# The second layer of the last two passes as one block product of seven half-size products

## The chip, the cores and the metric

The kernel runs on one core of a Trainium2 chip. The metric is the time of one execution on the device in microseconds. The core has five engines that run at the same time, each its own list of instructions in order: TensorE (PE, matmuls; its weight loads are shown as PEld), VectorE (DVE), ScalarE (ACT), GpSimd (POOL) and SyncE (SP, which here issues DMAs only). They work on an on-chip memory of 128 partitions (SBUF) and on the accumulators of TensorE (PSUM), and wait for each other by semaphores.

## The reference

Attention within clusters over 4 batches x 8 heads x 768 tokens x 64 columns, then a feed-forward network on 3072 tokens x 512 columns. All is float32.

```python
q_assign = argmax(einsum(q_n, c_n));  k_assign = argmax(einsum(k_n, c_n))    # 16 clusters
scores = where(q_assign == k_assign, scale * q @ k.T, -1e9)
attn_out = softmax(scores) @ v
x = attn_out.transpose(0, 2, 1, 3).reshape(3072, 512)
h = x @ w_in                                       # 512 -> 2048
g = maximum(h, 0) + log1p(exp(-abs(h)))            # softplus
out = g @ w_out                                    # 2048 -> 512
```

## The kernel before

Each float32 factor is held as two fp16 parts, high and low, and each product is three matmuls: high by high, high by low, low by high. The work is cut into eight passes of 384 tokens (three tiles of 128). Passes 6 and 7 are the two halves of the last batch. The attention runs some passes ahead of the feed-forward network, and fills the time up to about 730 us on all engines.

In the feed-forward network of a pass, `ffn1` makes one block of 128 columns of the hidden layer for all 384 tokens (16 blocks `f`, 12 matmuls 128x384 each, L1219 to L1221) in a PSUM buffer `h`, of which there are two. `softplus` takes it from there: exp and ln on ACT (`fa`, L1240, L1241), then one DVE instruction for the maximum with h (`fg`, float32, L1252), which also frees the `h` buffer. Two blocks share one `fg` tile of 768 columns. Its high part is cast into `gh` by ACT or POOL (helper `cast`, L298), its low part is `fg` minus the high part, on POOL or DVE (L1272). `ffn2` has 24 matmuls 128x512 (L1303 to L1305) for each token tile and each half of `f`, with `gh` as stationary and `wo` (the weights of the second layer, high and low) as moving factor, into the one PSUM buffer `o`. DVE evicts it to `ot` (L1347 for the first half, L1352 for the second, which adds), and SP stores the tile. The last tile of pass 7 is made in two halves of 256 columns, each evicted and stored by itself (`last_tile`, `last_store`, L1325 to L1336). Every matmul has a weight load of its own ahead of it.

The order of all instructions is written out by hand. The generators of the kernel (`ffn1`, `ffn2`, `softplus`, ...) are channels; each pair of characters in the table `PLAN` names the channel whose next instruction is emitted. The table `SWAPPED` lists the instructions that go to the second of two possible engines (`either`). Waits between channels (`wait`, `ring`) only say what may be emitted when; on the chip the semaphores decide.

```python
for pi in passes: for f in range(NF): ffn1(pi, f)                  # one channel
for pi in passes: for half in 0, 1: for i in range(QT): ffn2(pi, half, i)   # another
```

Of the kernel before, what the change touches and what calls it, by code (L numbers as in the profile page):

```python
# [38 lines left out]
SWAPPED = ('g0_3', 'g0_5', 'g1_1', 'g2_5', 'g6_6', 'g6_7', 'g7_1', 'g7_2', 'g7_4', 'g7_7', 'gh1_6', 'gh2_4', 'gh3_1', 'gh6_7', 'gh7_0', 'gh7_2', 'gh7_3', 'gh7_5', 'gh7_6', 'gh7_7', 'k0_0', 'k0_1', 'k14', 'k18', 'k22', 'kT0_0_0', 'kT0_2_1', 'kT1_2_0', 'kT1_2_1', 'm12_2_0', 'm12_3_0', 'm20_4_0', 'm8_2_0', 'm8_3_0', 'p100', 'p101', 'p103', 'p136', 'p38', 'p39', 'p40', 'p42', 'p45', 'p46', 'p47', 'p59', 'p61', 'p64', 'p67', 'p71', 'p72', 'p79', 'p82', 'p85', 'p89', 'p90', 'p92', 'ph58', 'ph62', 'ph83', 'ph86', 'ph87', 'q0_0_0', 'qT1_1', 'u1', 'u11', 'u13', 'u21', 'u23', 'u27', 'u31', 'u33', 'u35', 'v8', 'vh14', 'vh18', 'w15', 'w19', 'w20', 'w23', 'w29', 'wh17', 'wh24', 'wh29', 'wh30', 'wh7', 'wh9', 'x0_2', 'x2_0', 'xh0_3', 'xh1_3', 'xh2_3', 'xh3_0', 'xh3_3', 'zk10', 'zk12', 'zk16', 'zk18', 'zk2', 'zk20', 'zk4', 'zq0_1', 'zq8_2')  # L39
# [39 lines left out]
    "7d7d7d0x0x0x0x0x0x0x0x0xczfs117dfsfs10d0767dd0ft0zft78cz7aczfufufufud0cz11fufq7f7f7f7f7fczfv11727h7h7h7h7h7h"
    "cz7j7j7jfv7ccz7e7e7e7e7l7lfw7l7l7ld0fw7j7j7lfv7n7n7n7e7e7ed01111117pfwfwd07p7p7n7pfx11111111111111cz7r7rczfy"  # L80
    "fyfy7g7ncz7iczfz7rfz7t7t7t7t7p7pfw11d07vcz117x7t7r7rfzfzfz7v7v7k7xczg0g0g07m7t7x7x7xcz7z7z7oczg1g1g17v7vd0g1"
    "g17z818181818112d07q7x7q7q7q7q7q7q7z7zd0g2838383cz7sczg3g3g312127u81cz85858383czg48585857w878787g4g4g4878712"
    "czd089898989897y85g4d08bczg5g58bg58b8b8b80d08289fx8282828d8d8d8d8d13828282121212d08f8f8f8f8f12g684cz8h8h8h8h"
    "8hczg7g7g7868dg2d08j8j8j1212121212128j8j121313d088cz8a8hczg8g88l8l8l8lg8d0cz8cczg98e158e8e8n8n8e8l8ng7g78n8n"
    "czd0gacz15gbgbgbg9g912138gd0g9g98p168p8p8e8p8p158ld0czd0cz8i8pgcgc1616d0gd138r8r8r8r8rgc8e8ed08t8t8t8t8tgc13"
    "131313gccz8v8kcz8v8m8tgegege1313d0cz8oczgf8vgf8v8q178q8q148q131316gfgf8vgfcz8x8xczghghghd08z8z8x8x8x8xd0gi8s"
    "ggcz91918z8zgg8z14141418cz17gj8qgjgj919191d0939316161616161616d08u919595czgj939797gj93938q8q959595czgkgkgk18"
    "8wcz8y95czglglgl99d09797cz16gm16gm9bd0gngn909718179b99czgogogo9999d0921a189292929292czglgl999b14141414czgpgp"
    "gp9d9d9d1b9dczd099czgqgq141414149bgp141414141a9d9b1b1bd0cz94d0grgq969dczgsgsgsgsd01898d018181818181818gp1a9f"
    "9f9f9f9fcz9h9h9h9h9h9a1b9219gid0gt9j9j9j9j9j9cczgugu9e1c9h9e9e9e9e9egt9e9l9l9l9l9l9ld0gv9n9n191919gucz9p9pd0"  # L90
# [17 lines left out]


class Order:  # L110
    BEGIN = {"PE": 1500.0, "DVE": 1600.0, "ACT": 2400.0, "POOL": 2700.0, "SP": 1190.0}
    LAT = {"PE": 200, "DVE": 60, "ACT": 60, "POOL": 60, "SP": 0}

    def __init__(self):
# [68 lines left out]
def tile_cluster_attention__then__softplus_ffn(  # L183
# [1021 lines left out]
    def ffn1(pi: int, f: int):  # L1205
# [18 lines left out]
        if f == NF - 1:  # L1224
            od.set(xkey[pi])
# [180 lines left out]
```

## Time and profile before

| | us |
|---|---|
| median of 3 runs (825.67 to 825.87) | 825.8 |
| span of the profiled execution | 825.4 |
| TensorE busy in it | 809.5 (98%) |
| TensorE weight loads | 525.8 (64%) |
| ScalarE busy | 537.0 (65%) |
| VectorE busy | 522.1 (63%) |
| GpSimd busy | 458.7 (56%) |

The profile is of one execution. A row of it names the engine, the line of the kernel (L1219), the operation, output and inputs by the program's names, and shapes as partitions x elements. Matmuls are pipelined, so the duration of one is longer than the distance to the next; the pace of a stream is read from start to start. A DVE or POOL row shows when the instruction began and ended, any standing still inside it included.

### The profile page before, as it was taken

How to read it: one execution, taken by the hardware profiler on the slowest of the kernel's cores; microseconds unless marked ns; L12 is line 12 of the kernel's file. 1: busy time of each engine (PE TensorE's matmuls, PEld its weight loads, DVE VectorE, ACT ScalarE, POOL GpSimd, SP SyncE). 2: the span in 40 equal slices, each digit the busy share in tenths (PEclk: the TensorE clock that was granted, in tenths of full speed). 3: DMA queues.
4: the chain of work that ended last, by engine and by line, in shares of the span. 5: the costliest groups of instructions: out<-in, count | busy, mean ns of one | idle time of the engine just before them, and what ended most of it. 6: DMA issues, size and time to landing. Idle time of an engine off the chain costs nothing.

```text
span 825.4 us, 19143 instructions
## 1 busy us (share of the span) xinstructions
PE 809.5 (98%) x7919; PEld 525.8 (64%) x7919; DVE 522.1 (63%) x909; ACT 537.0 (65%) x830; POOL 458.7 (56%) x341
## 2 busy tenths in 40 slices
PE   7999999999999999999989999999999999999998
PEld 7888987655666666566656656556666656655554
DVE  6789998877876877666785557577555444332222
ACT  5776789865877777558578677767766668622220
POOL 4753556444756576655667685677576666611120
PEclk9999999999999999999999999999999999999999
DMA  8986768999999999998799999999889787530001
GB/s 236 239 197 138 204 158 218 213 212 197 179 177 174 179 207 201 212 197 170 153 166 172 183 171 208 199 197 172 171 158 163 136 138 134 118 54 14 26 1 39
DMA packets 389816, 133.69 MB, mean 162 GB/s; under 512 B 367072, under 2 KB 382688, under 8 KB 389728
## 3 DMA queue, kind: packets, MB, share of 16 engines
q1 hardware_dynamic: 389728, 132.46, 81.3%
q8 instruction: 62, 1.02, 0.5%
q14 instruction: 26, 0.21, 0.1%
HBM read 35.68 MB, written 6.29 MB: 51 GB/s over the span
## 4 chain that ended last, share of the span: by engine, by line
PE 86%; DVE 5%; DMA 4%; ACT 2%; issue 1%; POOL 0%; SPq 0%; DVEq 0%; ACTq 0%; POOLq 0%
PE s L1064 11%; PE h L1219 9%; PE h L1221 9%; PE h L1220 9%; PE o L1303 9%; PE o L1305 9%; PE o L1304 9%; PE mbank L1144 5%; PE mbank L1150 3%; PE mbank L1148 3%; PE mbank L1149 3%; DMA pt<-phl 2%; DMA kt<-kn 1%; PE u L996 1%; PE u L997 1%; PE m L957 1%
## 5 line engine op out<-in xcount | busy, mean ns | idle before, releaser
L1100 POOL TENSOR_TENSOR phl<-p,phl 128x768 f16<-128x768 f32 x133 | 220.3, 1664 | 145.5 <-ACT phl L298 98.8
L1080 DVE TENSOR_REDUCE negm<-s 128x1 f32<-128x768 f32 x156 | 148.3, 953 | 57.3 <-PE s L1064 57.0
L1086 ACT ACTIVATE p<-s,negm 128x768 f32<-128x768 f32 x156 | 139.5, 895 | 68.7 <-DVE negm L1080 56.4
L1221 PE MATMUL h<-xT,wi 128*128 128x384 f16 x512 | 166.8, 326 | 0.0
L1220 PE MATMUL h<-xT,wi 128*128 128x384 f16 x512 | 166.7, 326 | 0.0
L1219 PE MATMUL h<-xT,wi 128*128 128x384 f16 x512 | 166.7, 325 | 0.1
L1303 PE MATMUL o<-wo,gh 128*128 128x512 f16 x376 | 142.4, 379 | 0.4 <-DVE ot L1352 0.4
L1305 PE MATMUL o<-wo,gh 128*128 128x512 f16 x376 | 142.5, 379 | 0.0
L1304 PE MATMUL o<-wo,gh 128*128 128x512 f16 x376 | 142.4, 379 | 0.0
L298 ACT CAST phl<-p 128x768 f16<-128x768 f32 x151 | 123.8, 829 | 19.2 <-DMA pt<-phl 16.3
L1252 DVE SCALAR_TENSOR_TENSOR fg<-fa,h 128x384 f32<-128x384 f32 x128 | 70.1, 549 | 103.9 <-ACT fa L1241 95.9
L1240 ACT ACTIVATE fa<-h 128x384 f32<-128x384 f32 x128 | 62.3, 487 | 111.0 <-PE h L1221 110.6
L1064 PE MATMUL s<-kt,qt 128*128 128x384 f16 x624 | 127.0, 326 | 2.4 <-ACT p L1086 2.4
L1272 POOL TENSOR_TENSOR gh<-fg,gh 128x768 f16<-128x768 f32 x54 | 89.3, 1657 | 29.5 <-ACT gh L298 28.2
L1148 PE MATMUL mbank<-vb,pt 128*128 128x65 f16 x936 | 101.3, 192 | 0.5 <-DMA pt<-phl 0.5
L1149 PE MATMUL mbank<-vb,pt 128*128 128x64 f16 x936 | 101.4, 192 | 0.0
L1150 PE MATMUL mbank<-vb,pt 128*128 128x65 f16 x936 | 101.0, 194 | 0.0
L1148 PEld LDWEIGHTS <-pt 128*128 128x128 f16 x936 | 86.9, 98 | 14.2 <-DMA pt<-phl 2.6
L1149 PEld LDWEIGHTS <-pt 128*128 128x128 f16 x936 | 86.3, 97 | 11.4
L1150 PEld LDWEIGHTS <-pt 128*128 128x128 f16 x936 | 86.5, 97 | 0.0
L1064 PEld LDWEIGHTS <-qt 128*128 128x128 f16 x624 | 58.3, 98 | 43.2 <-issue 3.1
L1221 PEld LDWEIGHTS <-wi 128*128 128x128 f16 x512 | 49.9, 98 | 33.2
(180 smaller groups left out, 1307.3 us busy)
## 6 DMA issues: line engine op xcount, KB each, us to landing
wo<-in_moe_w_in_dram SPq DMA_DIRECT2D x16, 512.0 KB, 5.4
wo<-in_moe_w_out_dram SPq DMA_DIRECT2D x14, 512.0 KB, 4.3
out_dram<-ot SPq DMA_DIRECT2D x23, 256.0 KB, 2.6
rawk<-in_k_dram SPq DMA_DIRECT2D x15, 384.0 KB, 4.2
rawq<-in_q_dram SPq DMA_DIRECT2D x15, 384.0 KB, 4.4
rawv<-in_v_dram SPq DMA_DIRECT2D x12, 384.0 KB, 4.0
rawv<-in_v_dram SPq DMA_DIRECT2D x8, 192.0 KB, 6.1
pt<-phl SPq DMA_TRANSPOSE x78, 5.9
```

Of the source, the lines that this page charges most:

```text
L1064: nc.tensor.matmul(st[:, j, :SH], qt[:, s, i], kt[:, s, NT // 2 * j : NT // 2 * (j + 1)], start=(s == 0), stop=(s == 1),)
L1080: yield op("DVE", 950, lambda: nc.vector.tensor_reduce(negm, st[:, :, :SH], AX.XY, ALU.max, negate=True))
L1100: lambda e: e.tensor_tensor(phl[:, u, 1], p32, phl[:, u, 0], ALU.subtract),
L1148: nc.tensor.matmul(av, pt[:, 0, c], vb[:, c, D : 2 * D + 1], start=(c == 0), stop=False)
L1149: nc.tensor.matmul(av[:, :D], pt[:, 0, c], vb[:, c, :D], start=False, stop=False)
L1150: nc.tensor.matmul(av, pt[:, 1, c], vb[:, c, D : 2 * D + 1], start=False, stop=(c == NT - 1))
L1219: nc.tensor.matmul(hp, w[0], x[0], start=(c == 0), stop=False)
L1220: nc.tensor.matmul(hp, w[0], x[1], start=False, stop=False)
L1221: nc.tensor.matmul(hp, w[1], x[0], start=False, stop=(c == NP - 1))
L1303: nc.tensor.matmul(po, g[0], wo[:, f, 0, 0], start=(f == f0), stop=False)
L1304: nc.tensor.matmul(po, g[0], wo[:, f, 0, 1], start=False, stop=False)
L1305: nc.tensor.matmul(po, g[1], wo[:, f, 0, 0], start=False, stop=(f == f0 + NF // 2 - 1))
```

## The change

The second layers of passes 6 and 7 become one product of 2 x 2 blocks. The blocks of the activations are A11 (pass 6, f 0 to 7), A12 (pass 6, f 8 to 15), A21 and A22 (pass 7 likewise); the blocks of the weights are halves of f by halves of 256 output columns. Instead of eight block products there are Strassen's seven:

```
M1 = (A11+A22)(B11+B22)   M2 = (A21+A22) B11       M3 = A11 (B12-B22)   M4 = A22 (B21-B11)
M5 = (A11+A12) B22        M6 = (A21-A11)(B11+B12)  M7 = (A12-A22)(B21+B22)
C11 = M1+M4-M5+M7   C12 = M3+M5   C21 = M2+M4   C22 = M1-M2+M3+M6
```

PE does them in the order M3, M5, M4, M1, M7, M2, M6, each with 72 matmuls 128x256 (`product`): token tiles 0 and 1 first, then tile 2. Pass 7 makes the blocks 8 to 15 of its first layer ahead of 0 to 7 (`blocks`).

What is new beside this: the sums of activations (`sum5`, `sum1`, `sum7`, `sum2`, `sum6`: for each of four pairs of f a float32 sum of 768 columns, a cast for its high part and a subtraction for its low part); the sums of weights (`form3`, `form4`, `form1`, `form76`: for each pair of f of M3, M4, M1, M7, M6 three additions of 512 columns, a cast and a subtraction); and the evictions, in which each product goes with its sign into one or two of the blocks c11, c12, c21, c22 (`scaled`, `plus`), each of which is stored in two pieces (`send`). The sums live in buffers that the attention no longer uses by then: raw inputs, keys, queries, values, transposed p, and others. Only A11 and A22 still get a high and a low part of their own. `last_tile` and `last_store` are gone, and so are the old second layers of passes 6 and 7. `PLAN` and `SWAPPED` are new tables; the planner's times and costs are dropped, and the number of idle matmuls that fill PE's early gaps stands in a table `FILL`.

```diff
-        if f == NF - 1:
+        if f == (NF // 2 - 1 if pi == len(passes) - 1 else NF - 1):
             od.set(xkey[pi])
...
+    def add(key, ns, slow, dst, a, b, o=ALU.add):
+        return either(
+            key, ("DVE", ns), ("POOL", slow), lambda e: e.tensor_tensor(dst, a, b, o), shared=True
+        )
+
+    def parts(key, m, j, src):
+        hi, lo = S[m, j][:, 0], S[m, j][:, 1]
+        yield cast(f"{key}h_{j}", 830, 1290, hi, src)
+        yield add(f"{key}l_{j}", 950, 1640, lo, src, hi, ALU.subtract)
+        od.set(("A", m, j))
...
+    def sum7(j):
+        yield wait("sum", 5, j)
+        yield from six("qt", 2, ("last", "pt"), 7, j)
+        t = F[0, 1, j]
+        yield add(f"S7_{j}", 950, 1640, t, t, F[1, 1, j], ALU.subtract)
+        od.set(("sum", 7, j))
+        yield from parts("S7", 7, j, t)
+        od.set(tiles7[f"a12_{j}k"])
...
+    def form(m, j, a, b, o):
+
+        k = yield from ring("fg", 2)
+        t = flat(p2.tile([P, 2, nb], F32, tag="fg", name=f"t{m}_{j}"))
+        high = t[:, : 2 * HE].rearrange("p (u e) -> p u e", u=2)
+        low = t[:, 2 * HE : 3 * HE].bitcast(F16).rearrange("p (u e) -> p u e", u=2)
+        yield add(f"T{m}a_{j}", 640, 1160, high, a[0], b[0], o)
+        yield add(f"T{m}b_{j}", 340, 1160, low, a[1], b[1], o)
+        yield add(f"T{m}c_{j}", 640, 1160, high, high, low)
+        to = T[m, j]
+        yield cast(f"T{m}h_{j}", 655, 890, to[:, 0], high)
+        yield add(f"T{m}l_{j}", 640, 1160, to[:, 1], high, to[:, 0], ALU.subtract)
+        od.set(("T", m, j))
+        od.set(k)
...
+                    for u in range(2):
+                        x = [g[:, s, u, i * P : (i + 1) * P] for s in range(2)]
+                        first, last = i % 2 + j + u == 0, i > 0 and j == NJ - 1 and u == 1
+                        nc.tensor.matmul(to, x[0], t[0][:, u], start=first, stop=False)
+                        nc.tensor.matmul(to, x[0], t[1][:, u], start=False, stop=False)
+                        nc.tensor.matmul(to, x[1], t[0][:, u], start=False, stop=last)
...
+        for m in (1, 7, 2, 6):
+            key, x = yield from bank(ps_s, "s", 2, f"m{m}")
+            for w in range(2):
+                yield from product(m, w, x[:, w])
+                od.spawn(out41726(b, m, w, x[:, w], key if w else None))
...
-    def last_tile(pi, i):
-        b, c0 = passes[pi]
-        for e in range(2):
...
-    od.spawn((y for pi in range(len(passes)) for f in range(NF) for y in ffn1(pi, f)))
-    od.spawn((y for pi in range(len(passes)) for half in range(2) for i in range(QT) for y in ffn2(pi, half, i)))
+    od.spawn((y for pi in range(len(passes)) for f in blocks(pi) for y in ffn1(pi, f)))
+    od.spawn((y for pi in range(len(passes)) for y in (layer2(pi) if pi < R1 else seven(pi))))
+    for gen in (form3(), form4(), form1(), form76(), accs3()):
+        od.spawn(gen)
```

The order is the same in both kernels, on every engine, up to about 628.3 us of the trace. Behind it, VectorE's list in the second layer of pass 7 reads so before (`o_3_0_1` is the product of token tile 3 of batch 3, second half; `fg_7_2` the third pair of blocks of pass 7):

```order
L1252 SCALAR_TENSOR_TENSOR fg_7_2_11296<-fa_7_4_11292,h_7_4_11261 128x384
L1352 SCALAR_TENSOR_TENSOR ot_3_0_11118<-o_3_0_1_11253,ot_3_0_11118 128x512
L1252 SCALAR_TENSOR_TENSOR fg_7_2_11296<-fa_7_5_11325,h_7_5_11293 128x384
L1252 SCALAR_TENSOR_TENSOR fg_7_3_11360<-fa_7_6_11356,h_7_6_11326 128x384
L1352 SCALAR_TENSOR_TENSOR ot_3_1_11186<-o_3_1_1_11317,ot_3_1_11186 128x512
```

Each of these waits for PE or for ACT. After, at the fg rows of blocks 14 and 15 of pass 7, the list reads so (`pa2` is the pair of blocks in a dead buffer of transposed p; `s1_...` a sum or low part of M1's activations, `a12_2` the sum of M7, `t7_1` and `t1_3` sums of weights, `vb3` the place of M1's fourth block of weights, `c12` a block of the result):

```order
L1247 SCALAR_TENSOR_TENSOR pa2_11402<-fa_7_14_11458,h_7_14_11404 128x384
L1247 SCALAR_TENSOR_TENSOR pa2_11402<-fa_7_15_11472,h_7_15_11459 128x384
L1587 SCALAR_TENSOR_TENSOR c12_10936<-m35_11218,c22_10878 128x512
L1349 TENSOR_TENSOR s1_0_11337<-s1_1_11499,s1_0_11337 128x768
L1349 TENSOR_TENSOR vb3_110<-t1_3_11368,vb3_110 128x512
L1349 TENSOR_TENSOR a12_2_11039<-a12_2_11039,pa2_11402 128x768
L1349 TENSOR_TENSOR t7_1_11523<-kt1_11055,kt4_9918 128x512
L1349 TENSOR_TENSOR s1_2_11526<-na2_10548,pa2_11402 128x768
```

Between the fg rows there now stand rows of 128x768 and 128x512 whose inputs are both in SBUF. On GpSimd the list ended before with the parts of pass 7's activations:

```order
L298 CAST gh_7_6_11594<-fg_7_6_11554 128x768
L298 CAST gh_7_5_11525<-fg_7_5_11491 128x768
L1272 TENSOR_TENSOR gh_7_6_11594<-fg_7_6_11554,gh_7_6_11594 128x768
L1272 TENSOR_TENSOR gh_7_5_11525<-fg_7_5_11491,gh_7_5_11525 128x768
L298 CAST gh_7_7_11653<-fg_7_7_11649 128x768
```

After, it ends with sums and low parts of activations for M6 and M2 (`s6`, `s5`) and of weights for M6 (`t6`):

```order
L1349 TENSOR_TENSOR s6_0_11701<-ra0_10263,s6_0_11701 128x768
L276 CAST s5_0_10931<-pa0_11295 128x768
L1349 TENSOR_TENSOR s5_0_10931<-pa0_11295,s5_0_10931 128x768
L1349 TENSOR_TENSOR t6_1_11837<-kt1_11055,nt1_9616 128x512
L1349 TENSOR_TENSOR s5_2_11054<-pa2_11402,s5_2_11054 128x768
L1349 TENSOR_TENSOR t6_3_11928<-vb3_110,vb1_106 128x512
L1349 TENSOR_TENSOR t6_3_11928<-t6_3_11928 128x512
```

The subtractions and casts of pass 7's last pairs have left the list, and a sum that DVE and ACT go on with stands at its end.

## Rows read from the trace of the kernel before

**Rows 1.** The page, parts 1 and 2: busy us, share, instructions; 40 slices in tenths.
```profile
PE 809.5 (98%) x7919; PEld 525.8 (64%) x7919; DVE 522.1 (63%) x909; ACT 537.0 (65%) x830; POOL 458.7 (56%) x341
PE   7999999999999999999989999999999999999998
```
**Rows 2.** The page, part 4: the chain that ended last, by engine.
```profile
PE 86%; DVE 5%; DMA 4%; ACT 2%; issue 1%; POOL 0%; SPq 0%; DVEq 0%; ACTq 0%; POOLq 0%
```
**Rows 3.** Stretches: us, busy of PE, PEld, DVE, ACT, POOL; PE clock, DMA share, GB/s.
```profile
100.00:200.00 100.00, 99.47 (x932) 67.36 (x931) 82.20 (x149) 73.74 (x119) 48.76 (x39) 1.00 0.93 206
...
628.30:718.00 89.70, 89.70 (x871) 54.91 (x870) 41.64 (x67) 61.42 (x90) 54.21 (x35) 1.00 0.74 132
718.00:759.00 41.00, 41.00 (x279) 22.24 (x277) 11.26 (x19) 12.84 (x24) 8.75 (x8) 1.00 0.26 45
759.00:822.00 63.00, 63.00 (x348) 33.87 (x346) 14.65 (x23) 11.97 (x23) 9.51 (x8) 1.00 0.06 24
```
**Rows 4.** Timeline of PE, 800.9 to 822.4 us: start, duration, operation.
```profile
800.96 0.33 PE L1219 MATMUL h<-xT,wi 128*128 128x384 f16 x1
...
801.77 0.33 PE L1221 MATMUL h<-xT,wi 128*128 128x384 f16 x1
801.93 0.38 PE L1303 MATMUL o<-wo,gh 128*128 128x512 f16 x1
...
807.77 0.38 PE L1303 MATMUL o<-wo,gh 128*128 128x512 f16 x1
...
816.83 0.27 PE L1325 MATMUL o<-wo,gh 128*128 128x256 f16 x1
...
821.96 0.27 PE L1327 MATMUL o<-wo,gh 128*128 128x256 f16 x1
```
**Rows 5.** Timeline of DVE, its last row; in brackets the idle time before.
```profile
822.27 0.42 DVE L1335 SCALAR_TENSOR_TENSOR ot<-o,ot 128x256 f32<-128x256 f32 x1 [2.19 <-PE o L1327]
```
**Rows 6.** Timelines of ACT and DVE after that first-layer block.
```profile
802.13 0.49 ACT L1240 ACTIVATE fa<-h 128x384 f32<-128x384 f32 x1 [3.50 <-PE h L1221]
802.65 0.52 ACT L1241 ACTIVATE fa<-fa 128x384 f32<-128x384 f32 x1
...
803.27 0.56 DVE L1252 SCALAR_TENSOR_TENSOR fg<-fa,h 128x384 f32<-128x384 f32 x1 [4.04 <-ACT fa L1241]
```
**Rows 7.** Groups of DVE by shape, 740 to 825.4: count | busy us, mean ns | idle before.
```profile
L1252 DVE SCALAR_TENSOR_TENSOR fg<-fa,h 128x384 f32<-128x384 f32 x16 | 8.8, 553 | 33.4 <-ACT fa L1241 33.4
L1272 DVE TENSOR_TENSOR gh<-fg,gh 128x768 f16<-128x768 f32 x5 | 4.8, 957 | 4.9 <-ACT gh L298 4.6 <-POOL gh L298 0.4
L1352 DVE SCALAR_TENSOR_TENSOR ot<-o,ot 128x512 f32<-128x512 f32 x5 | 3.5, 692 | 15.5 <-PE o L1305 15.5
...
L1335 DVE SCALAR_TENSOR_TENSOR ot<-o,ot 128x256 f32<-128x256 f32 x2 | 0.8, 425 | 4.1 <-PE o L1327 4.1
```
**Rows 8.** Groups of DVE, then POOL, by shape: 128x512 and 128x768 subtractions, casts.
```profile
L426 DVE TENSOR_TENSOR wo<-wo 128x512 f16<-128x512 f32 x4 | 2.7, 684 | 0.0
...
L426 POOL TENSOR_TENSOR wo<-wraw,wo 128x512 f16<-128x512 f32 x2 | 2.3, 1160 | 1.9 <-ACT wo L298 1.8
...
L1272 POOL TENSOR_TENSOR gh<-fg,gh 128x768 f16<-128x768 f32 x15 | 24.6, 1644 | 4.5 <-ACT gh L298 3.3 <-PE o L1305 1.1
...
L298 POOL CAST gh<-fg 128x768 f16<-128x768 f32 x7 | 6.3, 909 | 65.2 <-DVE fg L1252 65.2
```
**Rows 9.** Timelines of DVE and POOL at 143 and 300 us; all of L1100 on DVE.
```profile
143.53 2.68 DVE L1100 TENSOR_TENSOR phl<-p,phl 128x768 f16<-128x768 f32 x3
...
300.41 2.12 DVE L1100 TENSOR_TENSOR phl<-p,phl 128x768 f16<-128x768 f32 x1
...
300.09 1.64 POOL L1100 TENSOR_TENSOR phl<-p,phl 128x768 f16<-128x768 f32 x1
...
L1100 DVE TENSOR_TENSOR phl<-p,phl x23: 943/956/2147, 143.5 to 508.1; 128x768 f16<-128x768 f32 x23
```
**Rows 10.** Groups of PE's weight loads, 816.8 to 822.3.
```profile
L1326 PEld LDWEIGHTS <-gh 128*128 128x128 f16 x16 | 1.6, 98 | 0.3
```
**Rows 11.** The tile pt (transposed p): time of its DMAs from issue to landing.
```profile
DMA to landing us min/median/max: 5.4/5.9/7.8
```

More of the change, by code (lines that the diff above doesn't have):

```diff
@@ L269, in tile_cluster_attention__then__softplus_ffn, with warm @@
     idle = mbank[:, 512 - WARM :]
-    def warm(gap):
-        if gap > WARM_FROM:
-            cold = min(gap * WARM_SHARE, max(0.0, COLD - cold_for[0]))
-            cold_for[0] += cold
-            for _ in range(int(cold / 100 + (gap * WARM_SHARE - cold) / 52)):
-                nc.tensor.matmul(idle, eye, ones[:, :WARM], start=True, stop=True)
-    cold_for = [0.0]
+    def warm(times):
+        for _ in range(times):
+            nc.tensor.matmul(idle, eye, ones[:, :WARM], start=True, stop=True)
     od.warm = warm
@@ L754, in prep_q @@
         n1 = p2.tile([P, c12, P], F16, name=f"qn1_{sfx}", **early)
+        if n == LAST - 3 and pi == len(passes) - 1:
+            od.set(("raws", "q"))
         if n == 0 and pi == 0:
@@ L797, in prep_q @@
             n2k, n2 = (yield from ring("n2", 1)), N2
+            if n == LAST - 3 and pi == len(passes) - 1:
+                od.set(("n2", "last"))
             if n == H:
@@ L1274, in softplus, with blocks @@
         )
-        od.set(fk)
-        od.set(("g", pi, fp))
+        if fk:
+            od.set(fk)
+        od.set(("g", pi, fp))
+        if pi == R1 + 1:
+            od.set(("A", 4, fp - NJ))
+            od.spawn(sum1(fp - NJ))
+            od.spawn(sum7(fp - NJ))
+        elif pi == R1:
+            od.set(("A", 3, fp))
+    R1 = len(passes) - 2
+    NJ = NF // 4
+    HE = DM // 2
+    def blocks(pi):
+        return list(range(NF)) if pi <= R1 else list(range(NF // 2, NF)) + list(range(NF // 2))
@@ new lines, in layer2, with flat, as_sum, as_form @@
+    def layer2(pi):
+        for half in range(2):
+            for i in range(QT):
+                yield from ffn2(pi, half, i)
+    F, S, T, tiles7 = {}, {}, {}, {}
+    def flat(ap):
+        n = len(ap.shape) - 1
+        axes = " ".join("abcde"[:n])
+        return ap.rearrange(f"p {axes} -> p ({axes})") if n > 1 else ap
+    def as_sum(ap):
+        return ap.rearrange("p (s u t) -> p s u t", s=2, u=2)
+    def as_form(ap):
+        return ap[:, : 4 * HE].rearrange("p (s u e) -> p s u e", s=2, u=2)
@@ new lines, in parts, with six @@
+    def parts(key, m, j, src):
[3 more added lines that the diff above has]
+        od.set(("A", m, j))
+    def six(tag, size, event, m, j, slots=2):
+        if j % 2 == 0:
+            yield wait(*event)
+            yield from take(tag, size, f"s{m}_{j}", [P, 4, 2 * nb], F16, **({"bufs": NP} if tag == "kt" else {}))
+            for u in range(2):
+                S[m, j + u] = as_sum(flat(tiles7[f"s{m}_{j}"][:, 2 * u : 2 * u + 2]))
+            od.set(("room", m, j))
+        else:
+            yield wait("room", m, j - 1)
@@ new lines, in form3 @@
+    def form3():
+        yield wait("raws", "q")
+        for u in range(2):
+            yield from take("n1", N1, f"nt{u}", [P, 6 * HE], F16, bufs=N1)
+            T[3, u] = as_form(tiles7[f"nt{u}"])
+        od.set(("form", "n1"))
+        yield wait("raws", "v")
+        for j in range(NJ):
+            if j >= 2:
+                yield from ring("vb", NP)
+                T[3, j] = as_form(flat(VB[j - 2]))
+            if j == NJ - 1:
+                od.set(("form", "vb"))
+            yield from form(
+                3, j, [weight(0, 1, j, s) for s in range(2)], [weight(1, 1, j, s) for s in range(2)], ALU.subtract
+            )
@@ new lines, in three, with form4 @@
+    def three(m, key):
+        for j in range(3):
+            T[m, j] = as_form(flat(tiles7[key])[:, 4 * HE * j : 4 * HE * (j + 1)])
+    def form4():
+        yield wait("kn", LAST - 1)
+        yield from take("kt", NP, "kt4", [P, 12 * HE], F16, bufs=NP)
+        three(4, "kt4")
+        od.set(("kt", 0))
+        yield wait("form", "vb")
+        yield from ring("vb", NP)
+        T[4, 3] = as_form(flat(VB[2]))
+        od.set(("form", "vb2"))
+        for j in range(NJ):
+            yield from form(
+                4, j, [weight(1, 0, j, s) for s in range(2)], [weight(0, 0, j, s) for s in range(2)], ALU.subtract
+            )
@@ new lines, in form1, with form76 @@
+    def form1():
+        yield wait("room", 5, 2)
+        yield from take("kt", NP, "kt1", [P, 12 * HE], F16, bufs=NP)
+        three(1, "kt1")
+        yield wait("form", "vb2")
+        yield from ring("vb", NP)
+        T[1, 3] = as_form(flat(VB[3]))
+        for j in range(NJ):
+            yield from form(
+                1, j, [weight(0, 0, j, s) for s in range(2)], [weight(1, 1, j, s) for s in range(2)], ALU.add
+            )
+    def form76():
+        yield wait("xT", len(passes) - 1)
+        yield from take("xT", 2, "xt7", [P, 12 * HE], F16)
+        three(7, "xt7")
+        yield wait("accs")
+        yield from take("ot", QT, "ot7", [P, 4 * HE], F16, bufs=QT)
+        T[7, 3] = as_form(tiles7["ot7"])
+        for m, other in ((7, 4), (6, 3)):
+            for j in range(NJ):
+                if m == 6:
+                    yield wait("done", 3)
+                    T[6, j] = T[3, j]
+                yield wait("T", 1, j)
+                yield wait("T", other, j)
+                yield from form(
+                    m, j, [T[1, j][:, s] for s in range(2)], [T[other, j][:, s] for s in range(2)], ALU.add
+                )
@@ new lines, in tile_cluster_attention__then__softplus_ffn, with span, scaled, emit @@
+    C = {}
+    def span(w):
+        return slice(0, 2) if w == 0 else slice(0, 1)
+    def scaled(key, dst, src, size, w):
+        def emit(e):
+            if e is nc.scalar:
+                e.activation(dst, src, AF.Copy, scale=size)
+            else:
+                e.tensor_scalar(dst, src, size, None, ALU.mult)
+        return either(key, ("ACT", 570 if w == 0 else 350), ("DVE", 680 if w == 0 else 360), emit)
+    def plus(dst, src, acc, w, sign=1.0):
+        return op(
+            "DVE",
+            360 if w else 680,
+            lambda: nc.vector.scalar_tensor_tensor(dst, src, sign / SW2, acc, ALU.mult, ALU.add),
+        )
@@ new lines, in send, with accs3 @@
+    def send(b, row, e, w, acc):
+        c0 = passes[R1 + row][1]
+        to = out_v[b, :, c0 : c0 + 2, e * HE : (e + 1) * HE] if w == 0 else out_v[b, :, c0 + 2 : c0 + 3, e * HE : (e + 1) * HE]
+        return op("SP", 60, lambda: nc.sync.dma_start(to, acc), dma=(128e3 if w else 256e3) / 290)
+    def accs3():
+        yield wait("last", "p32")
+        for r, e in ((2, 2), (1, 2), (1, 1)):
+            yield from take("p32", 3, f"c{r}{e}", [P, QT, HE], F32, bufs=3)
+            t = tiles7[f"c{r}{e}"]
+            C[r, e, 0], C[r, e, 1] = t[:, :2], t[:, 2:]
+            od.set(("c", r, e))
```

377 lines of the change are left out of this document (261 added, 116 removed).

## The prediction

> **What bounds the kernel now.** I read the page's busy shares and its 40 slices first: the reader is to see that TensorE (PE) is busy 98% of the span, in every slice but the first, and that no other engine is above 65% [rows 1]. The chain of the page's fourth part agrees: 86% of it is PE [rows 2]. Then the table of stretches, cut where the change cuts: instructions stand in the same order on every engine up to about 628.3 us, and from there to 822 us PE is busy without a gap, at a granted clock of 1.00 (the 2.4 GHz level), while VectorE (DVE) has 41.6 of 89.7 us, then 11.3 of 41.0, then 14.7 of 63.0 [rows 3]. So at the end PE alone sets the time and DVE is nearly idle. What the change takes from PE is gain, as long as what it gives to DVE fits. That is the whole question.
>
> **Term 1, PE.** The timeline of PE gives the pace of each shape, from start to start. First layer, 128x384: 801.77 − 800.96 over five steps, 0.162 us. Second layer, 128x512: 816.83 − 807.77 over 42 steps, 0.2157 us. The last tile, 128x256: 821.96 − 816.83 over 47 steps, 0.1091 us [rows 4]. Of the last two passes' second layers, before has 12 groups of 24 matmuls less the last tile's group, 264 x 0.2157 = 56.9 us, plus 48 x 0.1091 = 5.2, together 62.2 us. After has seven products of 72 matmuls 128x256: 504 x 0.1091 = 55.0 us. That is **−7.15 us** (seven eighths of the work, plus the fixed 2 x 109.1 − 215.7 = 2.5 ns that a halved matmul pays again). The 192 more matmuls bring 192 more weight loads; one takes 98 ns [rows 10] and lay hidden under the 109 ns matmuls of the last tile, so I cost them at nothing; uncovered they are a rival below. The end is of the same shape in both: last 128x256 group, one DVE eviction of 0.42 us, one store of 128 KB, end 3.44 us after the last matmul's start [rows 4, 5]. With PE never waiting the span would be 825.4 − 7.15 = 818.2 us.
>
> The Trainium skill, "TensorE: Matmul & The Clock Gate", section "Back-to-back issue gap", speaks against the change: it states that a stream of load and matmul pairs sustains about 131 ns at 512 columns and 81 ns at 128, where the load counts beside the columns. As an estimate on a line between these, 256 columns would take 98 ns, and the halving would cost 504 x 98 − (264 x 131 + 48 x 98) = +10 us. The trace has 215.7 and 109.1 ns for such streams [rows 4], so I go by the trace.
>
> **Term 2, what DVE must do, and with GpSimd (POOL).** From the place where the orders part, DVE has 106 instructions before (65.5 us by the prices below) and 222 after (156.6 us): the sums of activations (128x768) and of weights (128x512), and evictions into four blocks of the result. Prices: 128x768 with both inputs in SBUF 0.957, an fg row 0.553, a 128x512 eviction 0.692, a 128x256 one 0.425 [rows 7], a 128x512 subtraction 0.684 on DVE, 1.16 on POOL, where the 128x768 one takes 1.64 [rows 8].
>
> Two more readings of rows. Three 128x768 subtractions in a row took 2.68 us, not 3 x 0.956 = 2.87: independent DVE instructions overlap, 0.09 us for each after the first [rows 9]. And the subtraction at 300.41 took 2.12 us; POOL's own, begun at 300.09, ended at 301.73, and DVE's ended 0.80 later: it stood still while POOL worked, but for about 0.15 us [rows 9]. So such an instruction on one of the two engines stops the other.
>
> The stretch that decides runs from the fg row of block 15, the last of the eight first-layer blocks that pass 7 now does first (PE ends that block at 758.0 if it never waits), to the fourth block of weights of the last product, M6, which PE wants at 810.9. In it DVE has, by the order, 24 sums 128x768 (23.0 us), 25 of 128x512 (17.1), 8 fg rows (4.4), 5 large and 6 small evictions (3.5 + 2.6): **50.5 us**. With 0.09 off for some 60 of them, 45.1. POOL has nine instructions in it: 4 x 1.64 + 4 x 1.16 + one cast of 0.91 = 12.1 us; less 9 x 0.15 that is 10.8, and as 40.0 of DVE's 50.5 us (79%) are of the kind that is stopped, 8.5 us are added. DVE needs **53.6 us**. PE gives it 96 first-layer matmuls x 0.162 + 342 of the products x 0.1091 = 52.9, less 1.9 from the end of a first-layer block to the end of its fg row (exp, ln, DVE: 801.93 to 803.83 [rows 4, 6]), 51.0. So DVE comes **2.6 us late**, and PE waits for it in the last third, either before first-layer blocks (the ring of two PSUM buffers, freed by fg rows that stand in DVE's queue behind sums) or before M2 and M6. The bounds: if POOL takes nothing from DVE, not late (0); if nothing overlaps, 50.5 + 8.5 = 59.0, 8 late. I take the overlapped value, since the row with three such subtractions is the nearest to what stands there.
>
> The stretch before, 718 to 759 us, has 56 DVE instructions of 38.8 us, overlapped 34.5, with POOL's share 41.9 us, against 41.8 that PE gives: 0 to 0.7 late. From 628 to 718, the attention's end, DVE has 92 instructions of 64 us, about 76 of the 90 us with what POOL stops; the stretch 100 to 200 us of the trace had DVE at 82.2 and PE still at 99.47 of 100 [rows 3], so such a load costs PE some 0.5 us in 100. For both I take **+0.5**, bounds 0 and 4, the upper one because the transposes of p have a landing time of 5.4 to 7.8 us [rows 11] and their inputs now queue on DVE behind weight sums.
>
> Rest of the edits: the planner's constants removed and the idle matmuls from a table move nothing (200 of them in both); pass 7's blocks in another order cost nothing on PE; one result store more goes through SP in a stretch with a DMA share of 6% [rows 3]. Of the sums, those on ScalarE (casts) lie beside: 104 us of ACT in 190.
>
> **Sum.** Span 825.4 − 7.15 + 2.6 + 0.5 = 821.35. The median of the runs is 825.8, 0.4 above the profiled span, so **821.8 us**. The bounds of the terms: 818.2 + 0 + 0 and 818.2 + 8 + 4, that is 818.6 to 830.6 as times.
>
> **Rivals.** (1) *DVE keeps up*: POOL's instructions meet mostly DVE's waits, or PSUM evictions that they don't stop, so less than 5 of the 8.5 us are added. For it: PE had waits of nearly nothing with DVE at 82% [rows 3]. Against: here DVE would be needed for all of the 51 us. Time 818.6 to 819.5. (2) *Slower*: DVE becomes the bound outright. Most of the added instructions are chains in which the next reads what the last wrote (a + b, c + d, their sum, cast, low part), and each such step may wait for the end of the one before; then the full durations count, 59 us against 51, and 0.7 to 3 us come in the stretch before. PE loses 8 to 11 us, more than the 7.15 it saved; from 7.15 us of lateness on the change is a loss. Time 826.6 to 829.6, middle 828. For it: the place of DVE's instructions is fixed by the order, so a late cast stops everything behind it. Against: chains are interleaved in the order. (3) *The attention's end stalls*: the subtractions that make p's low part stand on DVE behind weight sums, transposes start later, PE waits for pt; 1 to 4 us over the forecast, 823 to 826. For it: the landing times [rows 11]. (4) *The change does not save what it says*: the pace at 128 x 256 rests on 48 matmuls; were the 98 ns load [rows 10] exposed for the 192 more, +18.8 us, 837. Against: those 48 [rows 4]. The skill's rule above belongs here.
>
> **How the numbers follow.** Chances: forecast (820 to 824) 0.46; rival 1 0.20; rival 2 0.18; rival 3 0.12; rival 4 0.02; 0.02 for anything else. About 0.2% (1.65 us) is what a measurement of this kernel can tell from no change: faster is below 824.1, slower above 827.5. Faster: 0.43 of the forecast + 0.20 + 0.04 of rival 3 = 0.67. Same: 0.03 + 0.06 of rival 2 + 0.08 of rival 3 = 0.17. Slower: 0.12 of rival 2 + 0.04 = 0.16. For 8 in 10 the range goes from just under rival 1, 818.0, to the middle of rival 2, 828.0: 0.1 lies above, and up to 0.1 below or in what I have not thought of.
>
> **What would show it.** Term 1: three lines of 168 matmuls each at 109 ns from start to start, and the same 3.4 us after the last. Term 2: PE idle of some 3 us between 740 and 811, its releaser the fg row or a sum on DVE, and DVE busy over 85% there; sums of 128x768 that last 1.1 to 2.1 us where POOL works. PE at 100% there would mean rival 1; PE idle of 7 us and more, with DVE's gaps in chains of weight sums, rival 2; PE idle before 718 with a DMA of pt as releaser, rival 3. The forecast is wrong at its root if PE waits for ScalarE's casts, which I cost at nothing.

## The result: slower, by waits for evictions

The changed kernel takes 833.5 us (median of six runs), the kernel before 825.4 us (median of six): a ratio of 1.0099, 95% interval 1.0085 to 1.0114. That is slower, and above the range of the prediction (818 to 828).

First the page of the changed kernel, busy times and three of the rows of 40 slices, which answer to [rows 1]:

```profile
PE 806.6 (97%) x8111; PEld 546.6 (66%) x8111; DVE 610.5 (73%) x1025; ACT 551.1 (66%) x854; POOL 472.0 (57%) x354
PE   8999999999999999999999999999999999999967
DVE  6788998877876877666765546586555778889973
PEclk9999999999999999999999999999999999999989
```

VectorE (DVE), 2 tenths busy at the end before, is now at 8 and 9 there, and TensorE (PE) has holes in the last slices. The table of stretches (length, then busy time of PE, weight loads, DVE, ACT, POOL, then PE's granted clock, DMA share, GB/s) answers to [rows 3]:

```profile
628.00:718.00 90.00, 90.00 (x869) 54.71 (x868) 67.89 (x96) 55.26 (x84) 53.92 (x42) 1.00 0.74 135
718.00:758.00 40.00, 40.00 (x348) 28.98 (x346) 36.31 (x55) 19.76 (x36) 15.10 (x12) 1.00 0.18 37
758.00:800.00 42.00, 39.79 (x313) 30.30 (x311) 40.62 (x55) 21.07 (x38) 11.41 (x7) 1.00 0.01 1
800.00:808.00 8.00, 1.03 (x8) 0.64 (x7) 7.25 (x10) 3.44 (x5) 3.18 (x2) 0.77 0.00 0
808.00:812.00 4.00, 4.00 (x24) 2.92 (x23) 0.61 (x2) 0.00 (x0) 0.00 (x0) 0.60 0.47 164
812.00:829.00 17.00, 14.84 (x136) 13.00 (x134) 7.05 (x10) 0.62 (x1) 1.74 (x1) 1.00 0.14 47
```

Up to 758 us PE is as full as before. From 758 to 800 it loses 2.2 us, from 800 to 808 nearly all, and behind that hole the granted clock is low (0.50, the 1.2 GHz level, from 807.3 to 811.2 us). The table of PE's waits from 628 us on (who waited for whom: total, times, longest) says for what:

```profile
PE m L1522 <- DVE c L1587: 9.1, 3, 7.0
PE h L1210 <- DVE fg L1247: 2.0, 3, 0.9
PE m L1524 <- DVE gh L1274: 0.2, 1, 0.2
```

The three large ones are waits of a product's matmul for an eviction (`c`, L1587). PE's timeline shows them at three places; in brackets the idle time before the row:

```profile
800.13 0.27 PE L1524 MATMUL m<-xt,s 128*128 128x256 f16 x1
807.37 0.37 PE L1522 MATMUL m<-xt,s 128*128 128x256 f16 x1 [6.97 <-DVE c L1587]
...
817.97 0.27 PE L1522 MATMUL m<-wo,s 128*128 128x256 f16 x1 [1.38 <-DVE c L1587]
...
826.77 0.27 PE L1522 MATMUL m<-nt,s 128*128 128x256 f16 x1 [0.78 <-DVE c L1587]
```

They are the products of token tile 2 of M7, M2 and M6. Their operands are there: `xt` and `s7` had served tiles 0 and 1 just before. What the matmul at 807.37 waits for is the row at 806.64 of DVE's timeline, the eviction of M7's tiles 0 and 1:

```profile
799.39 0.95 DVE L1349 TENSOR_TENSOR pa<-pa,fg 128x768 f32<-128x768 f32 x1
800.25 0.95 DVE L1349 TENSOR_TENSOR s<-pa,s 128x768 f16<-128x768 f32 x1
801.12 0.68 DVE L1587 SCALAR_TENSOR_TENSOR c<-m,c 128x512 f32<-128x512 f32 x1
801.75 1.71 DVE L1349 TENSOR_TENSOR nt<-t,nt 128x512 f16<-128x512 f32 x1
803.50 1.03 DVE L1349 TENSOR_TENSOR t<-kt,vb 128x512 f32<-128x512 f16 x2
804.56 0.69 DVE L1349 TENSOR_TENSOR t<-t 128x512 f32<-128x512 f32 x1
805.17 0.95 DVE L1349 TENSOR_TENSOR n<-fg,n 128x768 f32<-128x768 f32 x1
806.04 0.68 DVE L1349 TENSOR_TENSOR vb<-t,vb 128x512 f16<-128x512 f32 x1
806.64 0.68 DVE L1587 SCALAR_TENSOR_TENSOR c<-m,c 128x512 f32<-128x512 f32 x1
811.39 0.42 DVE L1587 SCALAR_TENSOR_TENSOR c<-m,c 128x256 f32<-128x256 f32 x1 [4.07 <-PE m L1524]
```

DVE has no gap of more than 0.04 us from 799.39 to the end of that eviction; the eviction comes when its turn comes, behind sums for M2 and M6, which PE makes only after M7. Each such product has one PSUM tile, token tiles 0 and 1 in its first half, tile 2 in its second. In PE's list of the changed kernel a wait for DVE (for a count of its semaphore `DVE_49`) stands ahead of the first matmul of tile 2 that the program issues after that eviction:

```
L1522 MATMUL m7_11814<-xt7_11175,s7_0_11338 128x256 [waits DVE_49]
L1522 MATMUL m2_11972<-wo_120,s5_0_10931 128x256 [waits DVE_49]
L1522 MATMUL m6_12057<-nt0_9615,s6_0_11701 128x256 [waits DVE_49]
```

For M2 and M6 that is the first matmul of tile 2, for M7 the seventh. The six ahead of it, the last at 800.13, stand before the eviction in the program and have no such wait: they write the second half while the first is still full.

**The account.** The first 600 us are the same list in both kernels, yet the traces differ by up to 2.6 us there from one execution to the next. So I count from a mark in the part that is common, the DVE row `negm` at 612.81 us of the kernel before, which stands at 613.00 in the changed one. From it to the end are 212.58 us before and 219.64 after, +7.1. The account: 7.15 us less work on PE; the waits above, 9.1 + 2.0 + 0.2 = 11.3; for each of the seven some 0.16 us more, since idle time counts from the modelled end of a matmul (0.27 us after its start) where the next could have started after 0.11, together 1.1; and the low clock, in these two rows of PE's timeline 3.20 us for 15 steps, 0.213 us where the others have 0.109, on 18 matmuls 1.9 us:

```profile
807.75 0.42 PE L1524 MATMUL m<-xt,s 128*128 128x256 f16 x1
...
810.95 0.40 PE L1524 MATMUL m<-ot,s 128*128 128x256 f16 x1
```

−7.15 + 11.3 + 1.1 + 1.9 = +7.2.

### The profile page after: what moved, and what is told of

The parts are those of the page before. It is cut to its first block, busy times and chain, and to the rows that moved or that the text cites. A ratio compares the mean times of both kernels' runs of the same rounds, so it can differ in the third digit from the quotient of the medians.

```text
span 832.6 us, 19674 instructions
## 1 busy us (share of the span) xinstructions
PE 806.6 (97%) x8111; PEld 546.6 (66%) x8111; DVE 610.5 (73%) x1025; ACT 551.1 (66%) x854; POOL 472.0 (57%) x354
## 4 chain that ended last, share of the span: by engine, by line
PE 59%; DVE 8%; DMA 6%; ACT 2%; issue 1%; POOL 0%; DVEq 0%; ACTq 0%; POOLq 0%
PE s L1051 9%; PE h L1212 7%; PE h L1210 7%; PE h L1211 7%; PE o L1674 6%; PE o L1676 5%; PE o L1675 5%; DMA pt<-phl 4%; PE mbank L1139 3%; PE mbank L1141 3%; PE mbank L1140 3%; DVE t L1349 1%; PE m L1522 1%; PE m L1524 1%; PE m L1523 1%; DVE s L1349 1%
## 5 line engine op out<-in xcount | busy, mean ns | idle before, releaser
L1089 POOL TENSOR_TENSOR phl<-p,phl 128x768 f16<-128x768 f32 x121 | 203.0, 1685 | 121.4 <-ACT phl L276 89.6
L1075 ACT ACTIVATE p<-s,negm 128x768 f32<-128x768 f32 x156 | 139.4, 896 | 65.3 <-DVE negm L1067 53.6
L276 ACT CAST phl<-p 128x768 f16<-128x768 f32 x144 | 117.9, 829 | 19.9 <-DMA pt<-phl 17.4
L1674 PE MATMUL o<-wo,gh 128*128 128x512 f16 x288 | 109.0, 379 | 0.2 <-DVE ot L1697 0.2
L1676 PE MATMUL o<-wo,gh 128*128 128x512 f16 x288 | 109.1, 379 | 0.0
L1675 PE MATMUL o<-wo,gh 128*128 128x512 f16 x288 | 109.1, 379 | 0.0
L1247 DVE SCALAR_TENSOR_TENSOR fg<-fa,h 128x384 f32<-128x384 f32 x104 | 56.7, 549 | 53.2 <-ACT fa L1232 45.8
L1274 POOL TENSOR_TENSOR gh<-fg,gh 128x768 f16<-128x768 f32 x42 | 70.1, 1670 | 25.2 <-ACT gh L276 25.1
```

The costliest lines, as they stand in the source:

```text
L1089: lambda e: e.tensor_tensor(phl[:, u, 1], p32, phl[:, u, 0], ALU.subtract),
L1674: nc.tensor.matmul(po, g[0], wo[:, f, 0, 0], start=(f == f0), stop=False)
L1675: nc.tensor.matmul(po, g[0], wo[:, f, 0, 1], start=False, stop=False)
L1676: nc.tensor.matmul(po, g[1], wo[:, f, 0, 0], start=False, stop=(f == f0 + NF // 2 - 1))
```

## The experiments

All runs, with the ratio of their times to those of the kernel before on the same chip, and the profiled execution counted from the mark (the kernel before had a median of 825.0 us beside the first four of the runs below, 825.3 beside the last three):

| run | median us | ratio, 95% interval | span | mark | mark to end |
|---|---|---|---|---|---|
| before | 825.4 | | 825.4 | 612.8 | 212.6 |
| changed | 833.5 | 1.0099, 1.0085 to 1.0114 | 832.6 | 613.0 | 219.6 |
| own_banks | 820.1 | 0.9941, 0.9923 to 0.9959 | 819.4 | 611.2 | 208.2 |
| m7_bank | 829.1 | 1.0050, 1.0033 to 1.0067 | 829.6 | 612.0 | 217.5 |
| no_sums | 820.7 | 0.9945, 0.9926 to 0.9964 | 819.5 | 610.8 | 208.7 |
| pool_fill | 826.6 | 1.0021, 1.0009 to 1.0034 | 826.2 | 610.4 | 215.7 |
| evict_first | 824.8 | 0.9996, 0.9979 to 1.0012 | 822.9 | 610.6 | 212.3 |
| fg_first | 820.2 | 0.9935, 0.9909 to 0.9960 | 818.6 | 611.2 | 207.4 |
| no_t76 | 823.1 | 0.9968, 0.9948 to 0.9988 | 824.4 | 612.1 | 212.3 |

**own_banks.** Nothing but the PSUM buffer of token tile 2 is another:

```diff
-                yield from product(m, w, x[:, w])
-                od.spawn(out41726(b, m, w, x[:, w], key if w else None))
+                po = x[:, w]
+                if w and m == 7:
+                    po = ps_o.tile([P, 1, HE], F32, tag="o", name="m7t")
+                elif w and m != 1:
+                    po = ps_h.tile([P, 1, HE], F32, tag="h", name=f"m{m}t")
+                yield from product(m, w, po)
+                od.spawn(out41726(b, m, w, po, key if w else None))
```

> Edit: the changed kernel, but the products of token tile 2 of M7, M2 and M6 go into PSUM buffers of their own (the one of o, the two of h), where the changed kernel puts them into the second half of the tile whose first half holds token tiles 0 and 1. Nothing else differs. Theory A (PE waits for evictions: the list of PE has a wait on DVE ahead of the tile-2 part of M7, M2 and M6, which is for the eviction of the first half of the same PSUM tile, and that eviction stands behind sums in DVE's queue): the waits of 7.0, 1.4 and 0.8 us go, and with them the clock drop that followed the long one (18 matmuls at 0.213 instead of 0.109 us, 1.9 us). Span 832.6 - 11.1 = 821.5, PE waits of some 2 to 3 us left ahead of first-layer blocks. Theory B (the sums themselves come too late, PE would wait for the operands of M2 and M6 anyway): the waits move to the first matmuls of M6 blocks, span 828 to 832.

All waits of PE from 628 us on:

```profile
PE h L1210 <- DVE fg L1247: 2.0, 3, 0.9
PE m L1524 <- DVE gh L1274: 0.2, 1, 0.2
```

Two stretches of the same run, with the columns as above:

```profile
758.00:800.00 42.00, 39.78 (x314) 30.36 (x313) 41.73 (x57) 20.84 (x37) 10.41 (x8) 1.00 0.00 1
800.00:816.00 16.00, 16.00 (x149) 14.34 (x147) 12.89 (x19) 2.70 (x4) 4.40 (x3) 1.00 0.26 89
```

The waits for evictions are gone, and the clock stays at 1.00. From the mark to the end it is 11.4 us less than in the changed kernel (11.1 expected), and the kernel is faster than both: 0.9941 of the one before. So theory A holds. DVE is as full as in the changed kernel up to 800 us (41.7 and 40.6 of 42); the sums are made in time for M2 and M6. So the wait costs the time, and the sums cost it only by what they keep waiting.

**m7_bank.** The same for M7 alone.

> Edit: as the run own_banks, but for M7 alone; M2 and M6 keep both parts in one PSUM tile. Theory A: the 7.0 us ahead of M7's tile-2 part go, PE ends M2's first part at about 807.3, and M2's evictions still stand behind five sums and low parts, until about 813: a wait of 4 to 6 us comes up ahead of M2's second part instead; span 827 to 831. Theory B: no change ahead of M2's second part beyond the 1.4 us, the wait stands ahead of M6; span 828 to 832.

The wait moved to the next eviction in the queue, M2's, as theory A has it, as PE's timeline shows:

```profile
812.47 0.37 PE L1522 MATMUL m<-wo,s 128*128 128x256 f16 x1 [5.83 <-DVE c L1590]
```

There the clock fell again, in the stretch behind it:

```profile
812.40:816.40 4.00, 3.93 (x19) 2.81 (x19) 0.01 (x1) 0.00 (x0) 0.00 (x0) 0.50 0.19 66
```

Mending one of three such waits gave back 2 of 11 us.

**no_sums.** PE's work without the sums:

```diff
-            key, ("DVE", ns), ("POOL", slow), lambda e: e.tensor_tensor(dst, a, b, o), shared=True
+            key, ("DVE", ns), ("POOL", slow), lambda e: None, shared=True
...
-                        x = [g[:, s, u, i * P : (i + 1) * P] for s in range(2)]
+                        x = [(g[:, s, u] if m in (3, 4) else wo[:, 2 * j + u, 0, s])[:, i * P : (i + 1) * P] for s in range(2)]
```

> Leaves out all sums of activations and weights with their casts and low parts; M1, M2, M5, M6 and M7 take slices of wo for both factors, M3 and M4 take real activations. Products, evictions, first layers and the order of the rest are the changed kernel's, PSUM tiles too. If the load on DVE is what makes evictions late (A and B alike), PE never waits long: the term of PE alone is left, 825.4 - 7.15 = span 818.2, at most 819.5 with the end's wait of 0.7 us ahead of M6's and M2's second parts. If the evictions' waits cost by themselves, whatever the load, span 823 or more.

PE's timeline has these waits and no others:

```profile
796.12 0.27 PE L1522 MATMUL m<-wo 128*128 128x256 f16 x1 [0.78 <-DVE c L1587]
...
804.86 0.27 PE L1522 MATMUL m<-wo 128*128 128x256 f16 x1 [1.38 <-DVE c L1587]
...
813.67 0.27 PE L1522 MATMUL m<-wo 128*128 128x256 f16 x1 [0.78 <-DVE c L1587]
```

With DVE busy for only 10.5 of the 42 us from 758 to 800, the same three waits are still there, each about as long as the eviction (one of 128x512 for M7 and M6, two for M2): 2.94 us. Against before, mark to end: −3.8 us, that is −7.15 + 2.94 + 3 x 0.16 = −3.7. The gain on PE is as worked out. The waits of M2 and M6 are the same in the changed kernel, 1.38 and 0.78 us, so that these two are the bare price of the shared tile; only M7's grew, from 0.78 to 6.97, and the low clock came behind it. From the mark own_banks, with all its sums, ends 0.5 us earlier than this kernel without any.

**pool_fill.** GpSimd's last nine two-input instructions become fills, which read nothing:

```diff
+        if key in ("S7l_0", "S7_3", "S6l_0", "S2l_1", "S2l_3", "T6a_1", "T6b_1", "T6a_3", "T6c_3"):
+            return op("POOL", slow, lambda: nc.gpsimd.memset(dst, 0.0))
```

> Edit: the changed kernel, but the last nine subtractions and additions of GpSimd (behind the block 15 of pass 7's first layer) are replaced by a fill of the same output with zero, which reads nothing; so the sums they make are left out. If GpSimd's two-input instructions stop DVE's (DVE rows of 2.20, 2.47, 3.10, 1.55, 1.58 and 1.71 us there, 7 us above their own durations up to 808): DVE comes to the eviction of M7's first half some 6 to 7 us earlier, the 7.0 us wait falls to 0 to 1 us with the clock drop, span 821 to 824. If those long rows have another cause, DVE's time and the wait stay, span 831 to 833.

The DVE rows that had lasted 2.2 us and the like have their own durations here, but for one pair beside a cast on GpSimd, so GpSimd was their cause. One of them in the changed kernel, and the same row here, which began within a fill (786.95 to 787.94):

```profile
793.68 1.55 DVE L1349 TENSOR_TENSOR pa<-pa,fg 128x768 f32<-128x768 f32 x1
787.34 0.96 DVE L1351 TENSOR_TENSOR pa<-pa,fg 128x768 f32<-128x768 f32 x1
```

The time that follows from it was missed:

```profile
PE m L1524 <- DVE c L1589: 7.4, 3, 5.2
```

M7's eviction starts at 799.47 (in the changed kernel 806.64), of which 2.6 us are the mark: 4.6 us earlier, not 6 to 7, as DVE now waits 1.2 us for ACT ahead of two fg rows. And PE comes earlier too, since its waits ahead of first-layer blocks went. A wait of 5.2 us was left, with its low clock. This much less time on DVE doesn't take the wait away while the eviction keeps its place.

**evict_first.** The order of DVE's list alone (32 pairs of `PLAN`); the lists of the other engines are the changed kernel's:

```diff
 L1247 SCALAR_TENSOR_TENSOR fg_3_11887<-fa_7_11880,h_7_11867 128x384
+L1587 SCALAR_TENSOR_TENSOR c_10878<-m_11651,c_10878 128x512
+L1587 SCALAR_TENSOR_TENSOR c_10950<-m_11814,c_10950 128x512
 L1349 TENSOR_TENSOR t_1_11837<-t_1_11837 128x512
...
-L1587 SCALAR_TENSOR_TENSOR c_10878<-m_11651,c_10878 128x512
...
-L1587 SCALAR_TENSOR_TENSOR c_10950<-m_11814,c_10950 128x512
 L1587 SCALAR_TENSOR_TENSOR c_10950<-m_11814,c_10950 128x256
+L1587 SCALAR_TENSOR_TENSOR c21p<-m_11972,c21p 128x512
+L1587 SCALAR_TENSOR_TENSOR c_10878<-m_11972,c_10878 128x512
```

> Edit: the changed kernel with its shared PSUM tiles; in DVE's list alone the evictions of M1's and M7's first part stand behind the fg rows of blocks 6 and 7, ahead of ten sums, and those of M2's first part ahead of five. No work is added or left out. If the place behind the sums is what made the eviction late, the 7.0 us wait falls to 1 us, M2's to 1 to 2 us, no clock drop, M6's 0.8 stays: span 823.5 to 825.5 at the early part of the changed kernel's trace (up to 2.5 us less with the early part of other runs). If DVE's total work is what counts, the sums that were passed make M2 or M6 wait as long: span 829 to 832.

All waits of PE from 628 us on:

```profile
PE m L1522 <- DVE c L1587: 3.6, 3, 2.0
PE h L1210 <- DVE fg L1247: 2.0, 3, 0.9
PE m L1524 <- DVE gh L1274: 0.2, 1, 0.2
```

9.1 us became 3.6 (0.8, 2.0 and 0.8) with all work and all shared tiles kept; the clock stayed at 1.00. Mark to end: 7.4 us less than the changed kernel. The span is 822.9, which would be 825.2 with the changed kernel's mark, within the 823.5 to 825.5 expected. So the place in DVE's list is what made M7's eviction late. The kernel is then even with the one before.

**no_t76.** The sums of weights of M7 and M6 left out.

> Leaves out the sums of weights of M7 and M6 (those products take slices of wo); all else as in the changed kernel, PSUM tiles too. DVE loses about 17 of its 51 us behind block 15. If evictions were late by DVE's load alone, it has slack now: the wait ahead of M7's tile-2 part falls from 7.0 to about 1 us, the waits of shared tiles stay at 0.7 to 1.4 each as in no_sums, no waits ahead of first-layer blocks; span 819.5 to 822.

This one was missed: PE still waits 2.8 us ahead of M7's tile 2. The rows of DVE ahead of it show why:

```profile
793.87 0.56 DVE L1247 SCALAR_TENSOR_TENSOR fg<-fa,h 128x384 f32<-128x384 f32 x1 [0.81 <-ACT fa L1232]
794.46 0.96 DVE L1349 TENSOR_TENSOR pa<-pa,fg 128x768 f32<-128x768 f32 x1
795.33 0.95 DVE L1349 TENSOR_TENSOR s<-pa,s 128x768 f16<-128x768 f32 x1
796.20 0.68 DVE L1591 SCALAR_TENSOR_TENSOR c<-m,c 128x512 f32<-128x512 f32 x1
796.80 2.01 DVE L1349 TENSOR_TENSOR n<-fg,n 128x768 f32<-128x768 f32 x1
798.74 0.68 DVE L1591 SCALAR_TENSOR_TENSOR c<-m,c 128x512 f32<-128x512 f32 x1
```

DVE has slack (it waits for ACT at 793), and the eviction still stands behind the last fg row and the four rows after it, one of them stopped by GpSimd. With DVE busy 32.8 instead of 40.6 of the 42 us between 758 and 800, 2.8 of 7.0 us are left; with all the work but a better place, in evict_first, M7's wait was 0.8.

**fg_first.** On top of own_banks, the fg rows of blocks 2 to 5 earlier in DVE's list, of which these are the first:

```diff
+L1247 SCALAR_TENSOR_TENSOR fg_1_11700<-fa_2_11676,h_2_11617 128x384
 L1349 TENSOR_TENSOR t_3_11679<-vb_110,vb_108 128x512 x2
+L1247 SCALAR_TENSOR_TENSOR fg_1_11700<-fa_3_11696,h_3_11677 128x384
 L1349 TENSOR_TENSOR t_3_11679<-t_3_11679 128x512
-L1247 SCALAR_TENSOR_TENSOR fg_1_11700<-fa_3_11696,h_3_11677 128x384
-L1247 SCALAR_TENSOR_TENSOR fg_1_11700<-fa_2_11676,h_2_11617 128x384
```

> Edit: the run own_banks, with the order table changed so that the fg rows of blocks 2, 3, 4 and 5 of pass 7 stand one to six DVE rows earlier (ahead of weight sums of M7 and M6), and the ln of block 5 two ACT rows earlier. Theory: of the 2.0 us that PE waits ahead of first-layer blocks in own_banks (0.3, 0.9 and 0.8), the last two go, since the fg rows wait for nothing but their place in DVE's list; the DVE work behind moves by some 2 us at most and is covered by PE's 150 matmuls ahead of M6. Span against own_banks at the same early part: 1.5 less. Rival: DVE is needed for all of its time there, what the fg rows gain the sums lose, and the wait comes up ahead of M2 or M6: no less than own_banks.

All waits of PE from 628 us on:

```profile
PE m L1522 <- DVE c L1592: 0.9, 2, 0.5
PE h L1210 <- DVE fg L1247: 0.3, 1, 0.3
PE m L1524 <- DVE gh L1274: 0.2, 1, 0.2
```

The two waits ahead of first-layer blocks went, as the theory has it; half of the gain came back as two waits for evictions (0.4 and 0.5 us), as the rival has it. 0.8 us are left of 1.5, counted from the mark; the medians of the two runs can't tell them apart. Both are faster than the kernel before and the changed one.

## Why the prediction was wrong

- **Term 1, −7.15 us on PE: right.** no_sums has it, and for the changed kernel and all seven runs −7.15 us, the waits from start to start and the low clock add up to the measured difference from the mark, to 0.2 us. 48 matmuls 128x256 of M2 run from 811.17 to 816.32 us at the pace of [rows 4], weight loads hidden; so rival 4 is out. The Trainium skill, "TensorE: Matmul & The Clock Gate", section "Back-to-back issue gap", would have made the halving a loss of 10 us, an estimate from its sustained figures. The trace of the changed kernel differs from that, at 0.109 us a matmul, as the one of before did, and the measurement decides.
- **Term 2, DVE late by 2.6 us: right in size.** In own_banks, where nothing else disturbs it, DVE needs 52.3 us from 758.15 to the end of M6's fourth block of weights at 810.41 (53.6 forecast). GpSimd's part, read in the changed kernel, is 8.0 us (8.5 forecast). PE waits 2.2 us, 2.0 of it ahead of first-layer blocks, a place that was named; with the modelled ends it loses 2.9. That this is so near to 2.6 is partly luck: by the prediction's own sum, 52.3 against 51.0 would be 1.3 late, and fg_first, by order alone, took 0.8 of the 2.9 away.
- **The stretches before, +0.5: zero.** PE is busy all of 628 to 758 us, with DVE at 67.9 of 90 and 36.3 of 40. Rival 3 didn't happen.
- **The step that failed** is the list of what PE can wait for, "either before first-layer blocks [...] or before M2 and M6". I looked for operands and for the ring of `h`, and counted the evictions as load on DVE alone. The change adds another wait, of the second half of a product on the eviction of its first half, and it was to be seen in PE's list ahead of the run. The three waits cost 9.1 us, 0.5 of modelled ends and 1.9 of clock: 11.4 by own_banks. 7.0 of the 9.1 are M7's alone, whose eviction stood behind the sums in DVE's list. Without these waits the forecast would have stood: from the mark own_banks is 4.4 us below the kernel before, where −7.15 + 2.6 + 0.5 = −4.05 was forecast.
- **Clock.** I took 1.00 throughout. It is 0.50 from 807.3 to 811.2 us, behind the 7.0 us wait.
- **Rival 2** had the sign and "a late cast stops everything behind it", but not the mechanism, nor the size: PE lost 14.3 us (9.1 + 2.0 + 0.2 + 1.1 + 1.9), not 8 to 11. Dependent DVE instructions didn't wait long: in the changed kernel a sum that reads the one before it started at 766.92, 0.03 us after that ended (766.48 + 0.41), and DVE's total came out nearer to the value with overlap (52.3 us, against 53.6 with it and 59.0 without).
- **From span to time.** I added 0.4 us. Every run here has 1.8 us or a little more between its span and its time, the kernel before too (823.1 and 825.0 in one of its runs). The profiled execution of before is one of the longer ones, by its first 600 us; comparing spans needs a mark in the common part.

Open is why the wait is there at all, as the two halves of the PSUM tile don't overlap. That it goes with a buffer of its own is shown, and M7's six matmuls without it ran while the first half was full. That the program's bookkeeping takes a tile as one is only argued.

## What to carry to other kernels

When a change gives an engine more work, look not only at its total but at the short instructions in its queue that another engine waits for: an eviction belongs ahead of sums that are needed later. Give two accumulations that are evicted apart a PSUM buffer each, and read the list of the waiting engine for waits that the code doesn't state. Work that nearly fits by its sum (DVE's 52.3 us against PE's 51.0 here) can still cost more than it saves by where it stands.

## What the runs showed of the hardware

The granted clock was at its lower level (0.50, 1.2 GHz) behind waits of PE of 7.0, 5.8 and 5.2 us (changed kernel, m7_bank, pool_fill), and at a mean of 0.60 over the 4.1 us behind the 2.8 us wait of no_t76. By PE's steps, longer there than the 0.109 us of the others, each such wait cost 1.5 to 2.5 us more than itself. Behind the 2.0 us wait of evict_first the clock stayed at 1.00. The stretches behind these last two waits, no_t76 first:

```profile
799.40:803.50 4.10, 4.03 (x23) 3.02 (x23) 0.33 (x2) 0.28 (x1) 0.00 (x0) 0.60 0.46 160
808.20:812.00 3.80, 3.79 (x35) 3.41 (x35) 3.80 (x5) 0.62 (x1) 1.74 (x1) 1.00 0.21 72
```

And a fill on GpSimd, which reads nothing, didn't stop DVE's sums with two inputs in SBUF (0.96 us beside it), where GpSimd's own sums did (1.55 us for the same row).
